# One transformer block, four edits at once: modulation weights as whole rows in a single first pass, value rows padded to 320 bytes, a reordered end of attention, and feed-forward weights in three slots queued by ScalarE

## The chip, the cores and the metric

The kernel runs on one core of a Trainium2 chip. The metric is device time in microseconds (us) of one execution; lower is better. Every number below comes from timed runs or from profiles (hardware traces of one execution). Engines: PE is TensorE (matrix multiply), PEld its weight loads, DVE VectorE, ACT ScalarE, POOL GpSimd, SP SyncE, which issues DMAs.

## The reference, cut to what matters

```python
mod = silu(c) @ w_mod            # c: 1x1024, w_mod: 1024x6144 -> sa, ca, ga, sb, cb, gb
h = layernorm(x) * (1 + ca) + sa # x: 2048x1024, bf16
x = x + ga * A(h)                # A: q = h @ wq (32 heads of 128), softmax(q k^T) v over the last
                                 #    512 cached keys (4 key heads, 8 query heads each), then @ wo
h = layernorm(x) * (1 + cb) + sb
x = x + gb * B(h)                # B: (silu(h @ w_gate) * (h @ w_up)) @ w_down, inner width 3584
```

The first product that needs `h` needs `sa` and `ca`, which are 2048 columns of `w_mod`: 4 MB that must arrive before the block can begin.

## The kernel before

Work is done in four chunks of 512 rows of x. Four parts matter here.

**The start.** The modulation columns come in two slices, and so does the first projection of four heads. `mod_slice` is 32 one-column matmuls per half slice; `x_mod` turns the transposed, normalized x into `hT`.

```python
# c arrives transposed, as 1024 pieces of 2 bytes
SP.dma_start(cT_bf[:, :], c.rearrange("o (k p) -> p (k o)", p=P))
...
for sl in range(2):
    load_wme(sl)          # four DMAs of 512 KB, runs of 1 KB
    load_wq0(sl)          # half of the first projection weights
...
for sl in range(2):
    if sl == 1:
        warm(4, SCB + 1); mod_slice(1, 0); warm(2, SCB + 1); mod_slice(1, 1)
        x_mod(1)
    for kc in range(sl * HK, (sl + 1) * HK):
        for h in range(LEAD + 1):
            mm(bank(QB0[h]), wq_s[0][:, kc, h*P:(h+1)*P], hT[0][:, kc, :], ...)
```

`warm(n, b)` is n matmuls of zeros, 512 columns each, whose result nobody reads: they keep PE's clock up.

**The heads.** For each head PE does 8 projection matmuls and 4 score matmuls of 512 columns, and 16 of 129 columns that multiply the exponentials with the value rows. A value row has 128 values and a 1 (for the softmax sum); the rows lie `VW` elements apart.

```python
VW = 130                                   # 260 bytes from row to row
v_aug = arena.at(OFF_VA, [GK, VW], BF16, [B_va])
...
mm(bank(b, P + 1, jj * 130), ex_s[es][:, kt, j*P:(j+1)*P],
   v_aug[:, gk * KT + kt, 0:P + 1], ...)   # 129 columns move through PE
```

**The end of attention.** When no projection is left to overlap, pieces of the last output projection fill in.

```python
if 0 <= i - 1 < NA: scores(i - 1)
n = i - (NA - LEAD)
if 0 <= n <= 2: oproj_mm(NCH - 1, 0, QB, 8 * n, 8 * n + 8)
elif n == 3:    oproj_mm(NCH - 1, 1, XB, 0, 12)
if 0 <= i - 2 < NA: pv(i - 2)
...
oproj(NCH - 1, 3)      # pieces 3 to 7, alternating between two PSUM banks
```

**Feed-forward weights.** Two slots of 2 MB (gate and up), queued by SP, in whose queue layer-norm transposes and output stores stand too.

```python
if jf % 4 == 1 and jf > 4:
    load_wgu(jf // 4 + 1)
gateup(jf)
```

The softmax here doesn't subtract the row's maximum and nothing guards it: scores larger than these inputs give would overflow.

## Time and profile before

1289.8 us median of 3 runs (1289.48 to 1290.48). One profiled execution spans 1289.0 us.

| stage | us from the start | what PE does |
|---|---|---|
| start | 0 to 31.4 | first work at 9.9, first projection in halves at 16.0 and 25.2, done at 30.5 |
| attention, four chunks | 31.4 to 657 | one head every 3.51 us |
| last output projection | 657 to 705 | 512-column matmuls |
| feed-forward | 705 to 1286 | 512-column matmuls |

The page's first part, busy time of each engine with its share of the span, says where to look:

```profile
PE 1263.4 (98%) x7636; PEld 648.3 (50%) x7778; DVE 447.5 (35%) x823; ACT 341.3 (26%) x384; POOL 37.3 (3%) x94
```

PE is busy 98% of the time, and the chain of waits puts 96% on one line of matmuls. So no other engine's speed matters by itself; there are the idle and the slow stretches of PE to win. The groups of instructions by shape (busy time, mean ns of one, idle before them and who ended it):

```profile
L266 PE MATMUL ps<-arena 128*128 128x512 bf16 x5084 | 1134.7, 380 | 11.7 <-DVE arena L467 2.2 <-DMA arena<-in_B_w_up_dram 0.8 <-ACT arena L620 0.7
L266 PE MATMUL ps<-arena 128*128 128x129 bf16 x2048 | 138.5, 220 | 1.1 <-DVE arena L641 1.1
```

A matmul is shown as 380 ns long although the chain steps on by 10.79 us for every 50 of them, 216 ns each: they overlap.

The timeline of PE at the start (start, duration, engine, line, operation; in brackets the idle time before and what ended it):

```profile
9.92 1.03 PE L270 MATMUL ps<-arena,nsc 128*128 128x128 bf16 x8 [9.92 <-DVE nsc L399]
...
16.00 5.47 PE L266 MATMUL ps<-arena 128*128 128x512 bf16 x19 [0.47 <-DVE arena L467]
21.31 0.94 PE L266 MATMUL ps<-sc_bf,arena 128*128 128x1 bf16 x32
22.33 0.38 PE L266 MATMUL ps<-arena 128*128 128x512 bf16 x1
22.55 0.94 PE L266 MATMUL ps<-sc_bf,arena 128*128 128x1 bf16 x32
25.20 5.30 PE L266 MATMUL ps<-arena 128*128 128x512 bf16 x16 [1.71 <-DVE arena L467]
30.34 1.06 PE L270 MATMUL ps<-arena 128*128 128x128 bf16 x16
```

The second half of the projection, 16 matmuls, takes 5.30 us instead of 16 x 0.216 = 3.5. The sums by stretch show why (for each stretch: length, busy time of PE, PEld, DVE, ACT and POOL with counts, granted TensorE clock, busy share of the DMA engines, GB/s):

```profile
10.00:16.00 6.00, 5.41 (x96) 5.20 (x98) 3.98 (x11) 1.73 (x2) 2.17 (x6) 1.00 1.09 385
16.00:22.00 6.00, 6.00 (x47) 2.84 (x47) 0.00 (x0) 0.96 (x2) 0.00 (x0) 1.00 1.09 382
24.00:28.00 4.00, 2.80 (x7) 1.04 (x8) 1.40 (x5) 1.45 (x2) 0.00 (x0) 0.66 0.68 162
```

In 24 to 28 us the granted clock is 0.66 of full speed. And the DMA runs flat at about 383 GB/s from 10 to 22 us.

The end of attention, timeline of PE:

```profile
640.02 14.64 PE L266 MATMUL ps<-arena 128*128 128x512 bf16 x112 [0.45 <-ACT arena L620]
655.75 14.03 PE L266 MATMUL ps<-arena 128*128 128x129 bf16 x74 [1.09 <-DVE arena L641]
670.16 42.05 PE L266 MATMUL ps<-arena 128*128 128x512 bf16 x190 [0.39 <-DVE tmp L660]
```

Three waits, 1.93 us. And in the feed-forward one wait, in the chain that ended last (start, duration, what):

```profile
1026.74 0.55 DVE nsc L399
1027.29 0.02 issue
1027.31 1.23 SPq L418
...
1028.63 0.53 SPq L767
...
1029.26 9.77 DMA arena<-in_B_w_up_dram
1039.03 0.04 issue
1039.08 6.00 PE ps L266 x27
```

SP stood at a layer-norm transpose (L418) until VectorE had made its input, and only then could it issue the gate and up weights behind it; the up weights landed at 1039.03, just too late for PE.

Lastly the pace of the heads, by two starts of a head's reciprocal on VectorE, six heads apart in the third chunk:

```profile
404.94 0.18 DVE L638 RECIPROCAL rl<-ps 128x4 f32<-128x4 f32 x1 [1.09 <-PE ps L266]
...
425.99 0.18 DVE L638 RECIPROCAL rl<-ps 128x4 f32<-128x4 f32 x1 [1.09 <-PE ps L266]
```

21.05 us for six: 3.51 us a head.

### The profile page before, as it was taken

The numbers are of one execution on the slowest core, as the hardware profiler recorded it, in microseconds if no ns is written. First come the engines' busy times: TensorE is split into PE (matmuls) and PEld (weight loads), VectorE is DVE, ScalarE is ACT, GpSimd is POOL, SyncE is SP. The second block draws the span as 40 slices with busy tenths as digits, with TensorE's granted clock in tenths as the row PEclk, the third lists the DMA queues.
The fourth block names the chain that finished last, engine by engine and source line by source line (L and its number), as shares of the span: only waits on it lengthen the run. The fifth ranks groups of instructions, "written<-read, shape, count | busy, mean of one in ns | idle before, by whom it ended". The sixth has DMA issues, their size and how long they took to land.

```text
span 1289.0 us, 17912 instructions
## 1 busy us (share of the span) xinstructions
PE 1263.4 (98%) x7636; PEld 648.3 (50%) x7778; DVE 447.5 (35%) x823; ACT 341.3 (26%) x384; POOL 37.3 (3%) x94
## 2 busy tenths in 40 slices
PE   6999999999999999999999999999999999999999
PEld 3565545665446554455544444444444444444444
DVE  3455424554136542265422331233222331221222
ACT  2555402555015551055520111011100111001100
POOL 1001200000000000000000000000000000000000
PEclk9999999999999999999999999999999999999999
DMA  8999701844105641055341683045410564044300
GB/s 263 311 222 295 218 1 25 193 103 106 34 9 127 143 104 45 1 125 114 70 152 33 194 296 130 17 149 162 149 56 28 151 206 131 17 136 142 131 9 25
DMA packets 212592, 155.33 MB, mean 120 GB/s; under 512 B 104736, under 2 KB 199840, under 8 KB 211488
## 3 DMA queue, kind: packets, MB, share of 16 engines
q1 hardware_dynamic: 212512, 154.17, 42.2%
q8 instruction: 61, 1.00, 0.3%
q14 instruction: 19, 0.16, 0.0%
HBM read 125.83 MB, written 4.19 MB: 101 GB/s over the span
## 4 chain that ended last, share of the span: by engine, by line
PE 97%; DMA 1%; issue 1%; DVE 1%; SPq 0%; ACT 0%; POOL 0%; DVEq 0%
PE ps L266 96%; DMA arena<-in_B_w_up_dram 1%; DMA x_res<-in_A_x_dram 0%; PE ps L270 0%; ACT arena L620 0%; DVE tmp L660 0%; DVE nsc L399 0%; DVE arena L467 0%; DVE st L388 0%; SPq L418 0%; ACT arena L489 0%; SPq L309 0%; DVE arena L641 0%; DVE x_res L662 0%; DVE rl L638 0%
## 5 line engine op out<-in xcount | busy, mean ns | idle before, releaser
L266 PE MATMUL ps<-arena 128*128 128x512 bf16 (+1 forms) x7204 | 1249.3, 333 | 12.8 <-DVE arena L467 2.2
L266 PEld LDWEIGHTS ps<-arena 128*128 128x128 bf16 x7346 | 634.0, 98 | 626.8 <-issue 7.1
L620 ACT ACTIVATE arena<-ps 128x1024 bf16<-128x1024 f32 x256 | 261.7, 1023 | 356.9 <-PE ps L266 345.2
L818 ACT ACTIVATE arena<-ps 128x512 bf16<-128x512 f32 x112 | 66.9, 597 | 515.6 <-PE ps L266 512.8
L819 DVE TENSOR_TENSOR arena<-ps,arena 128x512 bf16<-128x512 f32 x112 | 77.4, 691 | 277.4 <-PE ps L266 277.4
L660 DVE TENSOR_TENSOR tmp<-ps,rowb 128x512 f32<-128x512 f32 (+1 forms) x65 | 44.4, 683 | 320.5 <-PE ps L266 320.5
L571 DVE CAST arena<-ps 128x512 bf16<-128x512 f32 x124 | 85.7, 691 | 65.5 <-PE ps L266 65.5
L641 DVE TENSOR_TENSOR arena<-ps,rl 128x512 bf16<-128x512 f32 x128 | 88.5, 691 | 4.5
L638 DVE RECIPROCAL rl<-ps 128x4 f32<-128x4 f32 x128 | 23.3, 182 | 147.7 <-PE ps L266 147.7
L388 DVE BATCH_NORM_STATS2 st<-x_res 128x6 f32<-128x512 bf16 x62 | 42.4, 683 | 3.9 <-DMA x_res<-in_A_x_dram 3.8
L393 POOL TENSOR_SCALAR rstd<-mv 128x1 f32<-128x1 f32 x31 | 7.0, 227 | 952.8 <-DVE mv L392 941.4
L662 DVE TENSOR_TENSOR arena<-tmp,x_res 128x512 bf16<-128x512 f32 (+1 forms) x33 | 22.3, 676 | 1.1
L662 DVE TENSOR_TENSOR x_res<-tmp,x_res 128x512 bf16<-128x512 f32 x32 | 22.2, 692 | 1.1
L404 DVE TENSOR_SCALAR arena<-arena,gain,mod_bf 128x512 bf16<-128x512 bf16 x56 | 20.3, 405 | 0.0
L395 POOL TENSOR_TENSOR rstd<-rstd,mhalf 128x1 f32<-128x1 f32 x31 | 17.7, 573 | 2.6
L399 DVE TENSOR_SCALAR nsc<-x_res,mv,rstd 128x1024 bf16<-128x1024 bf16 x30 | 16.1, 536 | 2.1 <-POOL rstd L395 2.1
L270 PE MATMUL ps<-arena,nsc 128*128 128x128 bf16 x16 | 2.1, 311 | 10.0 <-DVE nsc L399 9.9
L266 PE MATMUL ps<-sc_bf,arena 128*128 128x1 bf16 x384 | 11.5, 164 | 0.0
L266 PEld LDWEIGHTS ps<-sc_bf,arena 128*128 128x128 bf16 x384 | 11.3, 97 | 0.5
L540 POOL TENSOR_SCALAR arena<-arena,c 128x128 bf16<-128x128 bf16 x16 | 9.7, 620 | 35.9 <-PE ps L266 35.7
L392 DVE BATCH_NORM_AGGREGATE mv<-st 128x2 f32<-128x12 f32 x31 | 6.5, 208 | 1.1
L270 PEld LDWEIGHTS ps<-arena,nsc 128*128 128x128 bf16 x16 | 1.5, 141 | 10.1 <-DVE nsc L399 10.1
(37 smaller groups left out, 30.8 us busy)
## 6 DMA issues: line engine op xcount, KB each, us to landing
arena<-in_A_wq_dram SPq DMA_DIRECT2D x31, 1024.0 KB, 6.0
arena<-in_B_w_gate_dram SPq DMA_DIRECT2D x28, 1024.0 KB, 5.4
arena<-in_B_w_up_dram SPq DMA_DIRECT2D x28, 1024.0 KB, 7.5
arena<-in_w_mod_dram SPq DMA_DIRECT2D x8, 1024.0 KB, 8.0
arena<-in_A_wo_dram SPq DMA_DIRECT2D x8, 1024.0 KB, 8.1
arena<-in_B_w_down_dram SPq DMA_DIRECT2D x7, 1024.0 KB, 6.3
arena<-in_w_mod_dram SPq DMA_DIRECT2D x8, 512.0 KB, 7.8
out_dram<-arena SPq DMA_DIRECT2D x15, 256.0 KB, 2.0
```

What stands on the lines that cost most here:

```text
L266: T.op(PE, lambda: TE.matmul(out_ap, lhsT, rhs, start=start, stop=stop, skip_group_check=skip), reads=reads, writes=[bank_buf])
L388: T.op(DVE, lambda: V.bn_stats(st_[sl][:, hf * 6:hf * 6 + 6], x_res[:, t, hf * 512:hf * 512 + 512]), reads=[B_x[t]], writes=[B_st[sl]])
L395: T.op(POOL, lambda: g.tensor_tensor(rstd[sl][:, :], rstd[sl][:, :], mhalf[:, 0:1], ALU.pow), reads=[B_rs[sl], B_mh], writes=[B_rs[sl]])
L404: T.op(DVE, lambda: V.tensor_scalar(dst[:, dt, :], dst[:, dt, :], gain[gi][:, dt:dt + 1], mod_bf[:, ccol + dt:ccol + dt + 1], op0=ALU.mult ...
L571: T.op(DVE, lambda: V.tensor_copy(qT_s[qs], bank(QB)), writes=[PB[QB], B_qT[qs]])
L620: T.op(ACT, lambda: A.activation(ex_s[es][:, 2 * kp:2 * kp + 2, :], banks2(SCB + 2 * kp), AF.Exp, scale=att_scale), writes=[PB[SCB + 2 * k ...
L638: T.op(DVE, lambda: V.reciprocal(rl[r][:, :].rearrange("p (a b) -> p a b", a=2), psap(PVB * 512 + P, [[512, 2], [130, 2]])), writes=both + ...
L641: T.op(DVE, lambda: V.tensor_tensor(o_s[os_].rearrange("p (a b) d -> p a b d", a=2), psap(PVB * 512, [[512, 2], [130, 2], [1, P]]), rlb, A ...
L660: T.op(DVE, lambda: V.tensor_tensor(tmp[s][:, 0:n], bank(b, n), rowb[ri][:, c0:c0 + n], ALU.mult), reads=[B_row[ri]], writes=[PB[b], B_tmp ...
L662: T.op(DVE, lambda: V.tensor_tensor(dst[:, c0:c0 + n], tmp[s][:, 0:n], x_res[:, t, c0:c0 + n], ALU.add), reads=[B_tmp[s], B_x[t]], writes= ...
L818: T.op(ACT, lambda: A.activation(sg_s[ss], bank(gb), AF.Silu), writes=[PB[gb], B_sg[ss]])
L819: T.op(DVE, lambda: V.tensor_tensor(guT[:, ft, :], bank(ub), sg_s[ss], ALU.mult), reads=[B_sg[ss]], writes=[PB[ub], B_gu[ft]])
```

## The change

Four edits, each with its own aim: let the first projection run in one piece at full clock with larger DMA runs; pad the value rows; fill the idle pieces at the end of attention; and fetch feed-forward weights a group earlier, out of SP's queue. The core of the diff, with cuts marked:

```diff
-    return SP.dma_start(cT_bf[:, :], c.rearrange("o (k p) -> p (k o)", p=P))
+T.op(Q_c, lambda: SP.dma_start(c_row[:, :], c.rearrange("o (k p) -> (o k) p", p=P)), writes=[B_cT])
+T.op(PE, lambda: TE.transpose(bank_bf(XB)[:, 0:DT], c_row[:, :], ident[0:DT, 0:DT]), ...)
 ...
+for k in range(DT):     # whole rows: runs of 4 KB
+    T.op(dq("q_wm%d" % k), lambda: SP.dma_start(wme[k], w_mod[k * P:(k + 1) * P, 0:NE * P]), ...)
-for sl in range(2):
-    load_wme(sl)
-    load_wq0(sl)
+load_wq0(0)
+load_wq0(1)
 ...
-VW = 130
+VW = 160
 ...                     # GpSimd's order: rstd of tiles 0 and 1 now ahead of tile 3's mean
+warm(9, WB)             # then stats, norm, x_first(0), warm(6), x_first(1), warm(2)
+for k in range(3):
+    mod_k(k)
+    warm(2, WB)
 ...
+mod_k(3)
+x_first(3)
+for k in range(4, DT):
+    warm(3, WB)
+    mod_k(k)
+warm(5, WB)
+x_mod()                 # all eight modulations, 5 on VectorE, 3 on ScalarE
 ...                     # the split in the first projection is gone
+n = i - (NA - LEAD)
+if 0 <= n <= 2:
+    oproj_mm(NCH - 1, 0, QB, 8 * n, 8 * n + 8)
+elif n >= 3:
+    oproj_mm(NCH - 1, 1, XB, 8 * (n - 3), 8 * (n - 3) + 8)
 if 0 <= i - 1 < NA:
     scores(i - 1)
-n = i - (NA - LEAD)     # was here, with 12 instead of 16 for piece 1
 ...
-oproj(NCH - 1, 3)
+for k, b in ((3, SCB + 1), (4, QB), (5, XB), (6, SCB + 2), (7, QB)):
+    oproj_mm(NCH - 1, k, b, 0, Hq)
+    oproj_end(NCH - 1, k, b)
 ...
-NWG = 2
+NWG = 3
-    T.op(Q_wg[sl], lambda: SP.dma_start(        # and the same for the up weights
+    T.op(Q_wg[sl], lambda: A.dma_start(
 ...
-if jf % 4 == 1 and jf > 4:
-    load_wgu(jf // 4 + 1)
 gateup(jf)
+if jf % 4 == 0:
+    load_wgu(jf // 4 + 2)
```

More of the change, by code (lines that the diff above doesn't have):

```diff
@@ L181, in bass_adaLN_cond__sliding_block_cached__swiglu_ffn__prompt_kernel @@
     mhalf = S_("mhalf", [P, TPC], F32)
-    cT_bf = S_("cT_bf", [P, DT], BF16)
+    c_row = S_("c_row", [DT, P], BF16)
     sc_bf = S_("sc_bf", [P, DT], BF16)
@@ L188, in bass_adaLN_cond__sliding_block_cached__swiglu_ffn__prompt_kernel @@
     nmean = S_("nmean", [P, 1], F32)
-    nmr = S_("nmr", [P, 1], F32)
     acc = S_("acc", [P, 2], F32)
@@ L232, in bass_adaLN_cond__sliding_block_cached__swiglu_ffn__prompt_kernel @@
     B_cT = _Buf("cT"); B_sc = _Buf("sc"); B_modbf = _Buf("modbf"); B_c6 = _Buf("c6")
-    B_mode = [_Buf("mode%d" % i) for i in range(2)]; B_gf = _Buf("gf")
-    B_nm = _Buf("nmean"); B_nr = _Buf("nmr"); B_acc = _Buf("acc")
-    B_g = [[_Buf("g0_%d" % i) for i in range(2)], [_Buf("g1")] * 2]
+    B_mode = _Buf("mode"); B_gf = _Buf("gf")
+    B_nm = _Buf("nmean"); B_acc = _Buf("acc")
+    B_g = [_Buf("g%d" % i) for i in range(2)]
     B_row = [_Buf("row%d" % i) for i in range(2)]
@@ L294, in _ @@
             T.op(POOL, lambda: g.memset(zwarm, 0.0), writes=[B_zw])
-            def dma_c():
-                with nc.allow_non_contiguous_dma(reason="tiny transposed c load"):
-                    return SP.dma_start(cT_bf[:, :], c.rearrange("o (k p) -> p (k o)", p=P))
             def load_x(ch):
@@ L306, in _ @@
             T.op(Q_x[0], lambda: SP.dma_start(x_res[:, 0, :], xf[0:P, :]), writes=[B_x[0]])
-            T.op(Q_c, dma_c, writes=[B_cT])
+            T.op(Q_c, lambda: SP.dma_start(c_row[:, :], c.rearrange("o (k p) -> (o k) p", p=P)), writes=[B_cT])
             for t in range(1, TPC):
@@ L326, in _ @@
             HK = DT // 2
-            B_wme = [[[_Buf("wme%d%d%d" % (sl, pt, kh)) for kh in range(2)] for pt in range(2)] for sl in range(2)]
-            wme = [[arena.at(OFF_OT + (2 * sl + pt) * 8 * KB, [DT, 512], BF16, B_wme[sl][pt]) for pt in range(2)] for sl in range(2)]
-            def load_wme(sl):
-                for kh in range(2):
-                    for pt in range(2):
-                        c0 = pt * D + sl * 512
-                        T.op(dq("q_wm%d%d%d" % (sl, pt, kh)), lambda: SP.dma_start(
-                            wme[sl][pt][:, kh * HK:(kh + 1) * HK, :],
-                            w_mod[kh * HK * P:(kh + 1) * HK * P, c0:c0 + 512].rearrange("(k p) n -> p k n", p=P)),
-                             writes=[B_wme[sl][pt][kh]])
+            B_wme = [_Buf("wme%d" % k) for k in range(DT)]
+            wme = [arena.at(OFF_OT + k * 4 * KB, [NE * P], BF16, [B_wme[k]]) for k in range(DT)]
+            for k in range(DT):
+                T.op(dq("q_wm%d" % k), lambda: SP.dma_start(wme[k], w_mod[k * P:(k + 1) * P, 0:NE * P]), writes=[B_wme[k]])
             NWQ = 2
@@ L378, in _ @@
                      writes=[B_vg[gk]])
-            T.op(POOL, lambda: g.memset(v_aug[:, :, P:VW], 1.0), writes=[B_va])
-            T.op(ACT, lambda: A.activation(sc_bf[:, :], cT_bf[:, :], AF.Silu), reads=[B_cT], writes=[B_sc])
+            T.op(POOL, lambda: g.memset(v_aug[:, :, P:P + 2], 1.0), writes=[B_va])
+            T.op(PE, lambda: TE.transpose(bank_bf(XB)[:, 0:DT], c_row[:, :], ident[0:DT, 0:DT]),
+                 reads=[B_cT, B_ident], writes=[PB[XB]])
+            T.op(ACT, lambda: A.activation(sc_bf[:, :], bank_bf(XB)[:, 0:DT], AF.Silu), writes=[PB[XB], B_sc])
             B_ns4 = B_ns + [_Buf("ns2"), _Buf("ns3")]
@@ L405, in modulate @@
                                                   mod_bf[:, ccol + dt:ccol + dt + 1], op0=ALU.mult, op1=ALU.add),
-                     reads=[B_g[gi][dt // HK], cbuf[dt // HK], bufs[dt]], writes=[bufs[dt]])
+                     reads=[B_g[gi], cbuf, bufs[dt]], writes=[bufs[dt]])
             def ln_task(ch, dst, bufs, gi, ccol, cbuf):
@@ L456, in x_first, with x_mod @@
                     transpose(bank_bf(dt // 2)[:, o:o + P], nsc4[t][:, dt * P:(dt + 1) * P], [B_ns4[t]], PB[dt // 2])
-            def x_mod(sl):
-                d0 = sl * HK
-                mod_read(d0, HK, 0, B_mode[sl])
-                mod_read(DT + d0, HK, HK, B_mode[sl])
-                mod_gain(0, d0, HK, B_mode[sl], B_g[0][sl])
-                T.op(DVE, lambda: V.tensor_copy(gain_f[:, d0:d0 + HK], gain[0][:, d0:d0 + HK]), reads=[B_g[0][sl]], writes=[B_gf])
-                for dt in range(d0, d0 + HK):
+            def x_mod():
+                T.op(DVE, lambda: V.tensor_copy(mod_bf[:, 0:NE], psap(XB * 512, [[2, NE]])), writes=[PB[XB], B_mode])
+                mod_gain(0, 0, DT, B_mode, B_g[0])
+                T.op(DVE, lambda: V.tensor_copy(gain_f[:, :], gain[0][:, :]), reads=[B_g[0]], writes=[B_gf])
+                for dt in range(DT):
                     src = bank_bf(dt // 2)[:, (dt % 2) * CH:(dt % 2 + 1) * CH]
-                    if dt % 2 == 0:
+                    if dt % 2 == 0 or dt == 5:
                         T.op(DVE, lambda: V.tensor_scalar(hT[0][:, dt, :], src, gain[0][:, dt:dt + 1], mod_bf[:, dt:dt + 1],
                                                           op0=ALU.mult, op1=ALU.add),
-                             reads=[B_g[0][sl], B_mode[sl]], writes=[PB[dt // 2], B_hT[0][dt]])
+                             reads=[B_g[0], B_mode], writes=[PB[dt // 2], B_hT[0][dt]])
                     else:
@@ L472, in x_mod, with mod_k, rstd_pow @@
                                                        bias=mod_bf[:, dt:dt + 1], scale=gain_f[:, dt:dt + 1]),
-                             reads=[B_gf, B_mode[sl]], writes=[PB[dt // 2], B_hT[0][dt]])
-            ECOLS = [(j, j) for j in range(HK)]
-            ECOLC = [(j, HK + j) for j in range(HK)]
-            def mod_slice(sl, kh):
-                for k in range(kh * HK, (kh + 1) * HK):
-                    for pt in range(2):
-                        w = wme[sl][pt]
-                        for j in range(HK):
-                            o = pt * HK + j
-                            mm(bank(XB, 1, 2 * o), w[:, k, j * P:(j + 1) * P], sc_bf[:, k:k + 1],
-                               k == 0 and o == 0, k == DT - 1, [B_wme[sl][pt][kh], B_sc], PB[XB], skip=True)
+                             reads=[B_gf, B_mode], writes=[PB[dt // 2], B_hT[0][dt]])
+            ECOLS = [(j, j) for j in range(NE)]
+            def mod_k(k):
+                mod_mm(wme[k], B_wme[k], k, ECOLS)
             tl = TPC - 1
+            def rstd_pow(t):
+                T.op(POOL, lambda: g.tensor_tensor(rstd[t][:, :], rstd[t][:, :], mhalf[:, 0:1], ALU.pow),
+                     reads=[B_rs[t], B_mh], writes=[B_rs[t]])
             T.op(ACT, lambda: A.activation(nsc4[tl], x_res[:, tl, :], AF.Copy, accum_out=acc[:, 0:1]),
                  reads=[B_x[tl]], writes=[B_ns4[tl], B_acc])
+            WB = PVB
+            warm(9, WB)
+            stats(0, 0, 0)
+            stats(0, 0, 1)
+            aggr(0)
+            stats(1, 1, 0)
+            norm(0, 0, 0)
+            x_first(0)
+            warm(6, WB)
+            stats(1, 1, 1)
+            aggr(1)
             T.op(POOL, lambda: g.tensor_scalar(nmean[:, :], acc[:, 0:1], -1.0 / D, None, op0=ALU.mult),
@@ L494, in _ @@
                  reads=[B_x[tl], B_nm], writes=[B_ns4[tl], B_acc])
-            stats(0, 0, 0)
-            stats(0, 0, 1)
-            aggr(0)
-            stats(1, 1, 0)
-            stats(1, 1, 1)
-            aggr(1)
-            norm(0, 0, 0)
-            x_first(0)
-            mod_slice(0, 0)
+            stats(2, 2, 0)
+            norm(1, 1, 1)
+            x_first(1)
+            warm(2, WB)
+            for k in range(3):
+                mod_k(k)
+                warm(2, WB)
+            stats(2, 2, 1)
+            aggr(2)
             T.op(POOL, lambda: g.tensor_scalar(rstd[tl][:, :], acc[:, 1:2], 1.0 / D, eps, op0=ALU.mult, op1=ALU.add),
                  reads=[B_acc], writes=[B_rs[tl]])
-            T.op(POOL, lambda: g.tensor_tensor(rstd[tl][:, :], rstd[tl][:, :], mhalf[:, 0:1], ALU.pow),
-                 reads=[B_rs[tl], B_mh], writes=[B_rs[tl]])
-            T.op(POOL, lambda: g.tensor_tensor(nmr[:, :], nmean[:, :], rstd[tl][:, :], ALU.mult),
-                 reads=[B_rs[tl], B_nm], writes=[B_nr])
-            T.op(ACT, lambda: A.activation(nsc4[tl], x_res[:, tl, :], AF.Identity, bias=nmr[:, 0:1], scale=rstd[tl][:, 0:1]),
-                 reads=[B_x[tl], B_nr, B_rs[tl]], writes=[B_ns4[tl]])
-            stats(2, 2, 0)
-            stats(2, 2, 1)
-            aggr(2)
-            norm(1, 1, 1)
-            x_first(1)
+            rstd_pow(tl)
             norm(2, 2, 2)
-            mod_slice(0, 1)
             x_first(2)
-            x_first(3)
-            x_mod(0)
+            warm(3, WB)
+            T.op(DVE, lambda: V.tensor_scalar(nsc4[tl], x_res[:, tl, :], nmean[:, 0:1], rstd[tl][:, 0:1],
+                                              op0=ALU.add, op1=ALU.mult),
+                 reads=[B_x[tl], B_nm, B_rs[tl]], writes=[B_ns4[tl]])
+            mod_k(3)
+            x_first(3)
+            for k in range(4, DT):
+                warm(3, WB)
+                mod_k(k)
+            warm(5, WB)
+            x_mod()
             NL = NJ - NE
@@ L576, in _ @@
             for sl in range(2):
-                if sl == 1:
-                    warm(4, SCB + 1)
-                    mod_slice(1, 0)
-                    warm(2, SCB + 1)
-                    mod_slice(1, 1)
-                    x_mod(1)
                 for kc in range(sl * HK, (sl + 1) * HK):
@@ L675, in oproj_end, with oproj @@
                 run_bg(1)
-            def oproj(ch, k0=0):
-                for k in range(k0, 2 * TPC):
+            def oproj(ch):
+                for k in range(2 * TPC):
                     b = [QB, XB][k % 2]
@@ L694, in add_ln2 @@
                     h2s[0] = arena.at(OFF_H20, [DT, CH], BF16, B_h2[0])
-                ln2[ch] = ln_task(ch, h2s[s], B_h2[s], 1, 3 * DT, [B_modbf] * 2)
+                ln2[ch] = ln_task(ch, h2s[s], B_h2[s], 1, 3 * DT, B_modbf)
                 bg.append(ln2[ch])
             LOADX = {3: 1, 19: 2, 40: 3}
-            LOADM = {1 + (3 * k) // 2: k for k in range(DT)}
+            LOADM = {(3 * k) // 2: k for k in range(DT)}
+            load_wml(0)
             MODM = {6 + (3 * k) // 2: k for k in range(DT)}
@@ L714, in _ @@
                         mod_read(NE, NL, 0, B_modbf)
-                        mod_gain(1, 0, DT, B_modbf, B_g[1][0])
+                        mod_gain(1, 0, DT, B_modbf, B_g[1])
                         for ri, jt in ((0, 2 * DT), (1, 5 * DT)):
@@ L730, in _ @@
                     qproj(i + LEAD)
-                if 0 <= i - 1 < NA:
-                    scores(i - 1)
                 n = i - (NA - LEAD)
@@ L735, in _ @@
                     oproj_mm(NCH - 1, 0, QB, 8 * n, 8 * n + 8)
-                elif n == 3:
-                    oproj_mm(NCH - 1, 1, XB, 0, 12)
+                elif n >= 3:
+                    oproj_mm(NCH - 1, 1, XB, 8 * (n - 3), 8 * (n - 3) + 8)
+                if 0 <= i - 1 < NA:
+                    scores(i - 1)
                 if 0 <= i - 2 < NA:
@@ L744, in _ @@
                 run_bg(1)
-            NWG = 2
+            NWG = 3
             OFF_WD = 0
-            OFF_G = [OFF_WQ, OFF_HT]
+            OFF_G = [OFF_WQ, OFF_HT, 56 * KB]
+            OFF_U = [OFF_WQ + 8 * KB, OFF_HT + 8 * KB, 144 * KB]
             OFF_GU = 96 * KB
@@ L755, in _ @@
             B_wu = [_Buf("wu%d" % i) for i in range(NWG)]
-            wg_s = [arena.at(OFF_G[i], [DT, 512], BF16, [B_wg[i]]) for i in range(NWG)]
-            wu_s = [arena.at(OFF_G[i] + 8 * KB, [DT, 512], BF16, [B_wu[i]]) for i in range(NWG)]
-            Q_wg = [dq("q_wg%d" % i) for i in range(NWG)]
-            Q_wu = [dq("q_wu%d" % i) for i in range(NWG)]
+            wg_s = [arena.at(OFF_G[i], [DT, 512], BF16, [B_wg[i]]) for i in range(2)]
+            wu_s = [arena.at(OFF_U[i], [DT, 512], BF16, [B_wu[i]]) for i in range(2)]
+            Q_wg = [dq("q_wg%d" % i, A) for i in range(NWG)]
+            Q_wu = [dq("q_wu%d" % i, A) for i in range(NWG)]
             FG = FT // 4
@@ L766, in load_wgu @@
                 sl = G % NWG
-                T.op(Q_wg[sl], lambda: SP.dma_start(
+                T.op(Q_wg[sl], lambda: A.dma_start(
                     wg_s[sl], B_w_gate[:, fg * 512:(fg + 1) * 512].rearrange("(k p) n -> p k n", p=P)), writes=[B_wg[sl]])
-                T.op(Q_wu[sl], lambda: SP.dma_start(
+                T.op(Q_wu[sl], lambda: A.dma_start(
                     wu_s[sl], B_w_up[:, fg * 512:(fg + 1) * 512].rearrange("(k p) n -> p k n", p=P)), writes=[B_wu[sl]])
@@ L774, in _ @@
             HL = Hq - 4
-            oproj_mm(NCH - 1, 1, XB, 12, HL)
+            oproj_mm(NCH - 1, 1, XB, 16, HL)
             oproj_mm(NCH - 1, 0, QB, 24, HL)
             oproj_mm(NCH - 1, 2, SCB, 0, HL)
-            for k, b in ((0, QB), (1, XB), (2, SCB)):
+            for k, b in enumerate((QB, XB, SCB)):
                 oproj_mm(NCH - 1, k, b, HL, Hq)
                 oproj_end(NCH - 1, k, b)
-            oproj(NCH - 1, 3)
+            for k, b in ((3, SCB + 1), (4, QB), (5, XB), (6, SCB + 2), (7, QB)):
+                oproj_mm(NCH - 1, k, b, 0, Hq)
+                oproj_end(NCH - 1, k, b)
             finish(ln2[0])
+            wg_s.append(arena.at(OFF_G[2], [DT, 512], BF16, [B_wg[2]]))
+            wu_s.append(arena.at(OFF_U[2], [DT, 512], BF16, [B_wu[2]]))
             B_h2[1] = [_Buf("h2_1_%d" % dt) for dt in range(DT)]
```

## The prediction

> **What bounds the kernel now.** TensorE. The page gives PE 1263.4 us busy of 1289.0 (98%), and the chain of waits is 96% matmuls of one line. In steady stretches the chain shows 10.79 us per 50 matmuls of 512 columns, 0.216 us each, and an attention head repeats every 3.51 us; the change touches neither. So only PE's idle and slow time can be won. The waits and the timeline show where it is:
> - Start-up. PE's first work comes at 9.9 us; its first transposes wait for the normalized tile, because GpSimd computes a value that needs x tile 3 before the reciprocal roots of tiles 0 and 1. The projection of the first four heads runs in two halves (16.0 and 25.2 us) and ends at 30.5 us. Between the halves PE does 64 one-column matmuls (about 1.9 us) and waits 1.7 us for VectorE. The second half starts at half clock: weight loads follow each other by 0.43 us, and the granted clock is 0.50 at 26 to 28 us, as the Trainium skill has it ("TensorE: Matmul & The Clock Gate", Part 1: idle PE falls to half rate).
> - DMA moves about 383 GB/s from 5 to 24 us, but only 30 GB/s in 3 to 4 us, where c lands as 2-byte pieces.
> - End of attention: PE idles 0.45 (exp), 1.09 (VectorE) and 0.39 us (residual).
> - Feed-forward: one wait of about 0.8 us for an up weight.
>
> **What changes.** c arrives as 8 rows. All 4 MB of the first modulation weights must land before any modulation. At 383 GB/s, behind 1 MB of x, I estimate the last row block at about 16.5 us. But TensorE's order then decides: from c's arrival (about 3.6 us) 9 warm matmuls at half clock (3.8 us), 29 at 0.216 (6.3 us), 128 one-column ones (32 take 0.9 us: 3.6 us), 32 transposes (1.8 us): about 19.1 us. Then the cast, gains and first VectorE modulation (1.5 us; 1.7 before) start the projection at about 20.6 us; 32 warm matmuls take 6.9 us: it ends near 27.5 us instead of 30.5. Gain 3.0 us; 5 if DMA, not the warm-ups, were the limit. The start of the attention loop (31.4 to 36.5 us before, with the exp table load) should move along unchanged.
>
> Output projection pieces moved in front of scores, 16 instead of 12 ahead of the last head, and more PSUM banks fill the three idle pieces: about 1.9 us. The third slot removes the 0.8 us. Issuing on ScalarE costs it about 1 us per four blocks of 3.45 us (an issue takes 0.5 us on SyncE); ScalarE is 11% busy there, so no loss. The skill ("DMA: Bandwidth & Descriptors", Issuing engines are not separate DMA queues) says that the engines are the same, so no bandwidth is gained; no trace here shows it yet. 320-byte value rows: nothing, since a head already runs at 3.51 us, nearly 12 x 0.216 + 16 x 0.056.
>
> **Sum.** 3.0 + 1.9 + 0.8 = 5.7 us: 1284.1 us, 80% range 1281.3 to 1287.0. Faster by over 2% 0.01, within 2% 0.97, slower 0.02.
>
> **Right or wrong.** In the profile after: first projection starts at 19.5 to 21.5 us, ends at 26.5 to 28.5 with the granted clock near 1; PE does not wait for modulation rows after the fifth; no idle of PE near 640, 655 and 670 us; no wait for an up weight; head period still 3.51 us.
>
> **What would break it.** Feed-forward weights on ScalarE's queue now start before the last output transposes and share the DMA engines with them; a late transpose would stall PE near 660 us. ScalarE stuck on a full queue would delay the SiLU. PE dropping to half clock between the modulation blocks. Rows landing later than the estimate.

## The result, and the profile after

1283.22 us median of 4 runs (1282.58 to 1284.60) against 1290.14 (1289.48 to 1290.63, 4 runs: the three above and one more). The ratio is 0.9948, 95% interval 0.9931 to 0.9965. Ratios here are the mean time of one kernel's runs over that of the other's of the same rounds, so not quite the ratio of the medians quoted. A ratio of 0.9948 at 1290 us is a gain of 6.7 us; 5.7 had been predicted, and the time lies within the stated range.

Busy time of each engine:

```profile
PE 1273.6 (99%) x7816; PEld 649.6 (51%) x7816; DVE 447.3 (35%) x820; ACT 339.4 (26%) x382; POOL 37.0 (3%) x93
```

The timeline of PE at the start:

```profile
3.72 3.49 PE L265 MATMUL ps<-arena 128*128 128x512 bf16 x9
...
18.33 0.54 PE L265 MATMUL ps<-sc_bf,arena 128*128 128x1 bf16 x16
18.73 1.24 PE L265 MATMUL ps<-arena 128*128 128x512 bf16 x5
20.25 7.15 PE L265 MATMUL ps<-arena 128*128 128x512 bf16 x32 [0.28 <-DVE arena L454]
27.24 1.06 PE L269 MATMUL ps<-arena 128*128 128x128 bf16 x16
```

The first projection starts at 20.25 and its 32 matmuls are through in 7.15 us, 0.22 each: full clock. The next work begins at 27.24 instead of 30.34. The same stretches as before:

```profile
10.00:16.00 6.00, 6.00 (x112) 4.26 (x110) 1.09 (x2) 0.10 (x2) 1.68 (x4) 1.00 1.02 412
16.00:22.00 6.00, 5.72 (x69) 2.99 (x68) 2.82 (x8) 1.44 (x2) 0.00 (x0) 1.00 1.09 352
24.00:28.00 4.00, 4.00 (x30) 2.23 (x29) 0.80 (x2) 0.56 (x1) 0.00 (x0) 1.00 0.99 243
```

While the modulation rows arrive (10 to 16 us) the DMA moves 412 GB/s instead of 385. (This trace holds no clock records, so its 1.00 for the clock is no evidence; the spacing of the matmuls is.)

From 86.56 us on PE never idles as far as the trace tells; one line of its timeline reaches over the whole of attention and into the feed-forward (the view ends at 720 us):

```profile
86.56 633.64 PE L265 MATMUL ps<-arena 128*128 128x512 bf16 x4292
```

So the three waits near 640, 655 and 670 us are gone in this execution, and no up weight is waited for later. (Six other traces have both the new end of attention and ScalarE's queue; in three of them a new, smaller wait stands near 660 us. See b_ffn.) And the heads' pace:

```profile
400.96 0.18 DVE L626 RECIPROCAL rl<-ps 128x4 f32<-128x4 f32 x1 [1.08 <-PE ps L265]
...
421.94 0.18 DVE L626 RECIPROCAL rl<-ps 128x4 f32<-128x4 f32 x1 [1.08 <-PE ps L265]
```

20.98 us for the same six heads (21.05 before): 3.497 us a head instead of 3.508. That is small, but there are 128 heads, and the prediction had said that this would not change.

Where this pair of traces differs, by the same event in both: 3.11 us at the first head's reciprocal (38.01 and 34.90), 4.61 at the 121st (632.16 and 627.55), 7.11 at the first product of the feed-forward (708.41 and 701.30), 8.25 at the end. So the start gave 3.1, the heads 1.5, the end of attention 2.5 and the feed-forward 1.1 us. That is 8.2 us where the timed runs show 6.7: one pair of traces can't be the whole story, and the experiments had to find which of these numbers belong to the change and which to that one execution.

### The profile page after: what moved, and what is told of

It is laid out like the page before. It is cut to its first block, busy times and chain, and to the rows that moved or that the text cites. A ratio compares the mean times of both kernels' runs of the same rounds, so it can differ in the third digit from the quotient of the medians.

```text
span 1280.8 us, 18074 instructions
## 1 busy us (share of the span) xinstructions
PE 1273.6 (99%) x7816; PEld 649.6 (51%) x7816; DVE 447.3 (35%) x820; ACT 339.4 (26%) x382; POOL 37.0 (3%) x93
## 4 chain that ended last, share of the span: by engine, by line
PE 99%; DVE 0%; ACT 0%; DMA 0%; issue 0%; POOL 0%; ACTq 0%; DVEq 0%
PE ps L265 98%; DMA x_res<-in_A_x_dram 0%; PE ps L269 0%; ACT arena L608 0%; DVE st L377 0%; ACT L608 0%; POOL rstd L384 0%; DVE nsc L388 0%; ACT arena L581 0%; POOL rstd L382 0%; DVE arena L454 0%; DVE mv L381 0%; DVE tmp L648 0%; DVE arena L650 0%; DVE mod_bf L448 0%
## 5 line engine op out<-in xcount | busy, mean ns | idle before, releaser
L265 PE MATMUL ps<-arena 128*128 128x512 bf16 (+1 forms) x7383 | 1264.3, 334 | 0.5 <-DVE arena L454 0.3
(39 smaller groups left out, 27.9 us busy)
```

Source lines behind the costliest of these rows:

```text
L265: T.op(PE, lambda: TE.matmul(out_ap, lhsT, rhs, start=start, stop=stop, skip_group_check=skip), reads=reads, writes=[bank_buf])
```

## The experiments

Twelve kernels ran, all with correct results. The first four put one part of the change alone into the kernel before; the four cuts add up to the whole change exactly. Medians below are beside runs of the kernel before on the same chip.

### b_start: the new start alone

Edit: the kernel before with c as rows, whole modulation rows, one pass, the warm matmuls and the early first late-modulation load; everything else as before.

> The kernel before with the new start alone (c as rows, whole modulation rows, one pass, warm matmuls, early first late-modulation load). Theory: the start is worth what the profile shows at the end of the first projection, 30.5 to 27.4 us, so the time falls by about 3.1 us and the head period stays 3.51 us. Rival (prediction's own alternative, DMA as the only limit): 5 us. If the start also shifts something later, the gain at the end of the program differs from the gain at 27 us.

Measured: 1287.53 us (1286.97 to 1287.78, 5 runs) against 1289.51; ratio 0.9983 (0.9970 to 0.9997), 2.2 us less. In its trace the first head's reciprocal is at 35.39 us, not 34.90. So I compared all traces, by that same event. With the old start: 38.01, 37.33, 36.57, 37.34, 38.79, 37.54 us, mean 37.6. With the new start unaltered: 34.90, 35.39, 34.85, 35.41, mean 35.1. The start is worth 2.5 us; the 3.1 of the first pair was a slow old start beside a quick new one. The rival's 5 us is out. One of nine runs of the kernel before shows a mean granted clock of 1.000 in place of 0.999, and it took 1287.18 us, 2.3 less than their median: a hint, from one run, that most of what the old start loses hangs on its 3.4 us at half clock. The pieces of the new start (c as rows, whole rows, one pass, warm matmuls, GpSimd's order) were not tried one by one; a_nowarm and a_1kb bear on two of them.

### b_pitch: 320-byte value rows alone

```diff
-VW = 130
+VW = 160
```

> The kernel before with 320-byte value rows alone. Theory: the attention-value matmuls run 0.8 ns faster each (57.5 to 56.7 ns), 2048 of them, so the head period falls from 3.51 to 3.50 us and the time by 1.6 us. Prediction on record: nothing, period stays 3.51. Rival: the shorter period in the changed kernel comes from somewhere else, and this run keeps 3.51.

Measured: 1288.80 us (1287.45 to 1288.97, 5 runs) against 1289.51; ratio 0.9992 (0.9979 to 1.0004): too small for the timing to show by itself. The trace shows it plainly. Its heads are 3.497 us apart, as in the changed kernel, and not 3.508; in b_start, b_tail and b_ffn, which keep 260 bytes, they stay 3.508 apart. From start to start its 129-column matmuls are 56.7 ns apart, all 16 of a head alike. In the kernel before, each value row serves two matmuls in a row, and on three rows out of four the first of the two is 59 to 61 ns from the second; the mean is 57.5 to 57.9. From the first head's reciprocal to the 121st it is 592.65 us here and in the changed kernel, and 594.15 or 594.16 in the kernel before and in b_start, b_tail and b_ffn: 1.5 us in 120 heads, 12.5 ns a head, 1.6 us for 128. The prediction's "nothing" fell here.

### a_mix: four row pitches in one kernel

Each of the four key heads has its own pitch, so that one execution compares them.

```diff
-VW = 160
-v_aug = arena.at(OFF_VA, [GK, VW], BF16, [B_va])
+VPITCH = [130, 132, 136, 160]      # 260, 264, 272, 320 bytes
+v_flat = arena.at(OFF_VA, [GK * 160], BF16, [B_va])
+def v_group(gk):                   # each group starts at a multiple of 1280 bytes
+    p = VPITCH[gk]
+    return v_flat[:, gk*640 : gk*640 + KT*p].rearrange("p (k w) -> p k w", k=KT)
```

> The changed kernel with another row pitch for the value rows of each key head: 260, 264, 272 and 320 bytes. Theory of 16 bytes: a value row that does not start at a multiple of 16 bytes costs about 4 ns at every second matmul; so the mean spacing of the attention-value matmuls is about 57.4, 57.0, 56.7 and 56.7 ns for the four (260: three of four rows off; 264: two of four; 272 and 320: none). Rival, whole 64-byte lines: 272 bytes is as slow as 260 (57.4) and only 320 is fast.

Measured (one look, 1283.38 us): mean spacing of the 129-column matmuls 57.5 ns at 260 bytes, 57.3 at 264, 56.7 at 272, 56.7 at 320. By row, what counts is where a row starts: rows 4, 8, 12 or 24 bytes into a 64-byte line cost 3 to 5 ns, rows 0, 16, 32 or 48 bytes into it cost nothing. So 16 bytes is the grain; whole 64-byte lines are out, and 272 bytes would have done as well as 320. The reciprocals of heads in the first group (260 bytes) and in the third (272), six heads apart:

```profile
380.23 0.18 DVE L632 RECIPROCAL rl<-ps 128x4 f32<-128x4 f32 x1 [1.09 <-PE ps L265]
...
401.27 0.18 DVE L632 RECIPROCAL rl<-ps 128x4 f32<-128x4 f32 x1 [1.09 <-PE ps L265]
...
436.29 0.18 DVE L632 RECIPROCAL rl<-ps 128x4 f32<-128x4 f32 x1 [1.08 <-PE ps L265]
...
457.27 0.18 DVE L632 RECIPROCAL rl<-ps 128x4 f32<-128x4 f32 x1 [1.08 <-PE ps L265]
```

21.04 us against 20.98. (264 bytes was expected at 57.0; its two bad rows cost nearly 5 ns each, a little more than a bad row at 260 bytes. Why was not tried.)

### b_tail: the end of attention alone

Edit: the reordered output projection and the additional banks, as in the diff above; the rest as before.

> The kernel before with the reordered output projection at the end of attention and the further PSUM banks alone. Theory: the idle pieces of 0.45, 1.09 and 0.39 us go, so 1.9 to 2.4 us less. Rival: they move elsewhere and less than 1 us is won.

Measured: 1287.14 us (1285.82 to 1288.41, 5 runs) against 1289.51; ratio 0.9980 (0.9968 to 0.9993), 2.6 us less. From the 121st reciprocal to the first feed-forward product: 73.81 us, against 76.25 in the kernel before and 76.26 in b_start. That is 2.44 us. PE's timeline in this stretch is one line, with no wait:

```profile
599.78 112.44 PE L266 MATMUL ps<-arena 128*128 128x512 bf16 x695
```

The predicted 1.9 was the sum of the idle times shown (0.45 + 1.09 + 0.39). The start-to-start distances at these places are 828, 1310 and 767 ns in place of 216, 57 and 216: 2.42 us lost. The difference is the 0.16 us by which a matmul's shown end lies behind the moment when the next could have started, once for each of three waits. The trace alone would have given the right number.

### b_ffn, b_ffn_sp3, b_ffn_act2: the feed-forward weights

b_ffn has three slots on ScalarE's queue in the kernel before. b_ffn_sp3 has the three slots but leaves them to SP; b_ffn_act2 has ScalarE's queue with two slots:

```diff
 # b_ffn_sp3: slots and place of issue
-NWG = 2
+NWG = 3
-if jf % 4 == 1 and jf > 4:
-    load_wgu(jf // 4 + 1)
 gateup(jf)
+if jf % 4 == 0:
+    load_wgu(jf // 4 + 2)
 # b_ffn_act2: the queue
-T.op(Q_wg[sl], lambda: SP.dma_start(
+T.op(Q_wg[sl], lambda: A.dma_start(
```

> The kernel before with the feed-forward weights in three slots queued by ScalarE alone. Theory: only the wait for the up weight near 1039 us goes (0.80 us of PE, 1.14 us in the VectorE products), so 0.8 to 1.2 us less; nothing lost near 660 us. Rival: the weights, now started before the last output transposes, delay these and some of it is lost.

> The kernel before with three weight slots in the feed-forward, still queued by SyncE. The smallest slack (first use of an up weight minus its landing) is -0.7 to 0.7 us in four traces with two slots on SyncE, and over 11 us in four with three slots on ScalarE. If the third slot makes the slack, it is over 8 us here; if the queue makes it, it stays under 3 us.

> The kernel before with two weight slots, queued by ScalarE. The least slack on SyncE belongs to weights issued right behind a layer-norm transpose that waits for VectorE (7 to 8 us late in the trace of before). If that queueing is the cause, ScalarE's queue alone lifts the smallest slack to 4 us or more with two slots; if only the third slot helps, it stays under 2 us.

Measured: b_ffn 1289.83 us (1289.04 to 1290.63, 5 runs) against 1289.51; ratio 1.0001 (0.9988 to 1.0013). No gain, although the trace of before shows 1.1 us lost at this place (matmul starts 1180 and 367 ns apart instead of 216). The other traces explain it. I took, for each group of weights, the time between the landing of the up weights and the moment PE needs them (the SiLU of the group's first block starts then). The smallest such slack in an execution:

| feed-forward weights | traces | smallest slack, us |
|---|---|---|
| two slots, SP (before, b_start, b_pitch, b_tail) | 4 | -0.72, 0.70, 0.45, 0.60 |
| two slots, ScalarE (b_ffn_act2) | 1 | 0.01 |
| three slots, SP (b_ffn_sp3) | 1 | 14.6 |
| three slots, ScalarE (b_ffn, after) | 2 | 13.4, 12.5 |

The old scheme is always on the edge and fell off it in one of four executions, the one shown in the profile before. The length of the feed-forward says the same: from its first product to the end of the program 580.62 us in the profile before, 579.48 in b_start, b_pitch and b_tail, and 579.48 in b_ffn. So the gain is about 1.1 us now and then, not in every run. The third slot alone makes the slack. ScalarE's queue alone does not (the second of the two outcomes that I had expected): it does help the weights that stood behind a transpose (group 17: 4.0 us instead of 0.7 or less), but the tightest ones are then groups 3 and 4, whose loads run beside those of the down weights, and at group 4 PE waited a little (453 ns between starts in place of 216).

The rival came true in part. b_ffn has no new wait near 660 us, but with ScalarE's queue the last transpose of the attention output takes 8.2 us to land, and 2.4 in the kernels that leave the weights to SP: the weights now start before it. With the old end of attention there is room for that. The new end leaves less: in the seven traces that have it together with ScalarE's queue (the changed kernel and all runs named a_) this transpose takes 8.7 to 9.5 us, and in three of them (a_mix, a_nowarm, a_1kb) PE waits for it, 504, 712 and 607 ns between starts in place of 216, so 0.3 to 0.5 us. From the chain of a_nowarm that ended last (start, duration, what):

```profile
653.82 9.46 DMA arena<-arena
663.27 0.05 issue
663.32 0.82 PE ps L265 x3
```

Three slots left to SP together with the new end of attention would have kept both the slack of 14.6 us and the transposes of 2.4 us, as far as b_ffn_sp3 and b_tail tell; that kernel was not run.

### a_fewwarm, a_nowarm: what sets the start

```diff
 # a_fewwarm (in a_nowarm, all seven warm() calls go)
 for k in range(4, DT):
-    warm(3, WB)
+    warm(1, WB)
     mod_k(k)
```

> The changed kernel with 1 instead of 3 warm matmuls before each of the last four modulation row blocks (8 fewer, 1.7 us of PE). Theory of the prediction, TensorE's queue sets the start and DMA has slack: the first projection starts 1.7 us earlier, at 18.5 us, and the time falls by 1.7. Rival, seen in the trace after (last row block lands at 18.0 us, first projection weights at 19.5): at most 0.3 us earlier, with TensorE now waiting for the last row blocks.

> The changed kernel with no warm matmul at all. Theory: the projection starts no later (about 20 us) but at half clock: weight loads 0.43 us apart for some 3 to 4 us, 32 matmuls in 8.5 to 9 us instead of 7.15, so its end and the time are 1 to 2 us later than the changed kernel. Rival, the warm matmuls only fill time: same time within 0.3 us.

a_fewwarm: 1283.54 us (1281.54 to 1284.31, 4 runs), ratio 0.9953 (0.9936 to 0.9969): no gain over the changed kernel's 0.9948. In its trace the projection starts at 19.18, 1.0 us earlier: between the two theories. But in that execution the last row block happened to land at 16.98 us; in the changed kernel's trace at 18.01, where PE took it up at 18.33. So TensorE's queue and the DMA are near each other, and which ends later differs from run to run.

a_nowarm: 1284.82 us (1284.76 to 1285.05, 4 runs), ratio 0.9961 (0.9946 to 0.9976), about 1.6 us slower than the changed kernel, as expected. The projection starts at 20.72 and takes 8.39 us, since PE runs at half clock: weight loads 0.43 us apart until 23.7 us. (Start, duration and idle time of PEld:)

```profile
22.43 0.15 PEld L265 LDWEIGHTS ps<-arena 128*128 128x128 bf16 x1 [0.27 <-issue]
22.86 0.15 PEld L265 LDWEIGHTS ps<-arena 128*128 128x128 bf16 x1 [0.28 <-issue]
23.29 0.15 PEld L265 LDWEIGHTS ps<-arena 128*128 128x128 bf16 x1 [0.28 <-issue]
```

So the warm matmuls do not only fill time. In this trace the first head's reciprocal is at 36.61 us, 1.5 later than the mean of 35.1 with them and only 1.0 earlier than the old start's 37.6; another 0.5 us went at 663 us (the transpose above).

### a_1kb: the same modulation block in 1 KB runs

```diff
-for k in range(DT):
-    SP.dma_start(wme[k], w_mod[k * P:(k + 1) * P, 0:NE * P])
+for k in range(0, DT, 4):
+    for n in range(4):
+        SP.dma_start(wme_all[:, k:k + 4, n * 512:(n + 1) * 512],
+                     w_mod[k * P:(k + 4) * P, n * 512:(n + 1) * 512].rearrange("(k p) n -> p k n", p=P))
```

> The changed kernel with the same modulation block fetched as eight pieces of 1 KB runs (four row blocks by 512 columns) instead of eight whole row blocks of 4 KB runs. Theory: the longer runs raise the DMA rate in this stage from about 385 to 412 GB/s, so here the last piece lands 0.7 to 1.5 us later than 18.0 us and the projection starts that much later. Rival: the rate doesn't depend on the run length, the last piece lands at 18.0 within 0.3 us; the start may still move a little because row blocks 0 to 3 arrive together.

Measured: 1287.34 us (1286.49 to 1287.59, 4 runs), ratio 0.9979. The last piece lands at 19.45 us; in seven traces with whole rows the last one lands at 16.98 to 18.78 us, mean 18.05. From 10 to 16 us:

```profile
10.00:16.00 6.00, 3.53 (x60) 2.25 (x58) 1.09 (x2) 0.08 (x1) 1.68 (x4) 0.93 1.09 349
```

349 GB/s against 412: fetched this way the block comes more slowly, and lands 1.4 us later, as expected. But the rate is not the 385 that the theory had taken from the kernel before, where the runs are 1 KB too. Packets of 1 KB take 46 ns there and 51 ns here, so the length of the runs is not all of it. In the kernel before, a piece lands in one stretch of 4 KB per partition, here in four of 1 KB that lie 4 KB apart. No run separates these causes. The projection starts at 24.84, 4.6 us later, and only 1.4 of that is the landing: TensorE waits 1.14 and 1.25 us for pieces early on, loses its clock, and all the warm matmuls behind them in its queue are late as well. So this run shows a lower rate, not what the higher rate is worth.

### a_same and a_best: a try at a better start

a_same is the changed kernel again. a_best takes a_fewwarm and moves the float copy of the gains behind the first two modulations:

```diff
+# for dt in range(DT): in x_mod
+    if dt == 2:
+        T.op(DVE, lambda: V.tensor_copy(gain_f[:, :], gain[0][:, :]), ...)
-    if dt % 2 == 0 or dt == 5:      # on VectorE
+    if dt % 2 == 0 or dt == 1:
```

> The changed kernel once more, unaltered, to be timed beside the next run and to show how far one execution's start differs from another's. Expected: 1283 us; the first projection starts at 20.2 us, or later if the last modulation rows land after 18.3 us (one of four traces so far: 18.8 us, start at 20.7).

> The changed kernel with 1 instead of 3 warm matmuls before each of the last four row blocks, and with the first two modulations on VectorE ahead of the float copy of the gains (0.2 us off the chain from the last row block to the projection). Theory: the start now follows the last row block's landing (17.0 to 18.8 us so far) by 1.8 us instead of TensorE's queue, so 0.3 to 1.0 us less than the changed kernel in the mean, 1282.4. Rival: the projection's own weights, landing at 19.0 to 20.3 us, bind as well and less than 0.3 us is won.

Measured in the same rounds: a_same 1283.08 us (1282.61 to 1283.59, 5 runs), ratio 0.9946 (0.9932 to 0.9959); a_best 1284.40 us (1282.21 to 1285.58, 5 runs), ratio 0.9955 (0.9942 to 0.9967). Not better: one run is faster than all of a_same's, but four are slower, and they spread over 3.4 us instead of 1.0. Its trace shows how the theory failed. PE's timeline:

```profile
15.93 0.54 PE L265 MATMUL ps<-sc_bf,arena 128*128 128x1 bf16 x16
18.26 0.59 PE L265 MATMUL ps<-sc_bf,arena 128*128 128x1 bf16 x16 [1.78 <-DMA arena<-in_w_mod_dram]
18.71 10.95 PE L265 MATMUL ps<-arena 128*128 128x512 bf16 x36
29.50 1.06 PE L269 MATMUL ps<-arena 128*128 128x128 bf16 x16
```

The last row block landed at 18.21 us. With so few warm matmuls left PE had nothing to do for 1.78 us, its clock fell, and the five warm matmuls and the projection then ran at half clock (weight loads 0.43 us apart until 24.5 us). The projection ended near 29.7 instead of 27.9 us in a_same. The clocks of the five timed runs bear this out: 1282.21 us at a mean granted clock of 1.000, 1283.73 and 1284.40 at 0.999, 1284.84 and 1285.58 at 0.997. The three warm matmuls per row block are a bridge over late rows: they cost about 1 us when the rows are early (a_fewwarm's trace, 19.18 against 20.25) and save nearly 2 us when they are late. The changed kernel stands; no version that was timed here beats it.

## Why the prediction was right or wrong

The sum was right: 5.7 us predicted, 6.7 measured, inside the range. The terms, against their parts alone:

| part | predicted | shown by traces | timed alone |
|---|---|---|---|
| start | 3.0 | 2.5 (3.1 in the first pair) | 2.2 |
| value rows | 0 | 1.6 | 1.0 (interval -0.5 to 2.7) |
| end of attention | 1.9 | 2.4 (0.3 to 0.5 less in three of the seven traces that also have ScalarE's queue) | 2.6 |
| feed-forward weights | 0.8 | 1.1 in one execution of four | -0.1 |
| sum | 5.7 | 6.5 without the last | 5.7 |

- **What bounds the kernel** was right: everything gained is idle or slow time of PE, and PE's share went from 98% to 99%.
- **The start** was right in its times: predicted start of the projection 20.6 and end 27.5 us; measured 20.25 and 27.4. Its reasoning was half right. It had the last row block landing at 16.5 us, with DMA far ahead of TensorE's queue and 5 us to be had if DMA were the limit. It landed at 18.0 in that trace. TensorE took it up at 18.33, and in other executions it landed at 17.0 to 18.8. Both limits lie within about a microsecond of each other, so trimming the queue gains nothing (a_fewwarm, a_best).
- **"320-byte value rows: nothing"** was the step that failed. It reads "a head already runs at 3.51 us, nearly 12 x 0.216 + 16 x 0.056". That sum is 3.488; the missing 22 ns a head were called nothing, and 128 heads make 2.8 us of them. About 12.5 ns of them, 1.6 us in all, were rows off a multiple of 16 bytes. The rest was rounding: with the measured 56.7 and 215.8 ns the sum is 3.497, which is the head period after.
- **The end of attention** was right in its mechanism; the size was the sum of the idle times shown, 1.93, in place of the 2.42 us between starts.
- **The feed-forward wait** was read as a property of the kernel. It was a property of one execution of a kernel with slack near zero. The third slot is a good guard, but worth little in the mean. That ScalarE's issuing costs nothing was right within the noise: b_ffn is not slower. No bandwidth was gained either: the median up weight took 7.5 us to land in b_ffn as before (8.4 in the changed kernel), and the transposes beside the weights landed later, as the Trainium skill has it ("DMA: Bandwidth & Descriptors", Issuing engines are not separate DMA queues): whoever issues, the DMA engines are the same.
- **"A late transpose would stall PE near 660 us"**, the first item under what would break it, did not happen in the profile after, but did in three of the seven traces with the new end and ScalarE's queue, at 0.3 to 0.5 us each. So the fear was right in its mechanism, and the profile after happened to be one of the four without it. The head period, predicted to stay at 3.51, is the one item of the list "right or wrong" that came out wrong in that profile.

Errors in opposite directions (1.6 us too little for the value rows, 0.8 too much for the feed-forward, half a microsecond each way for the other two) largely cancelled, which is luck; the right total does not vouch for the terms.

## What to carry to other kernels

Take PE's loss from the distance between starts of matmuls, not from the idle time shown, and don't round off a gap per head or per tile before multiplying it by their number. Lay rows that move through TensorE at a multiple of 16 bytes (shown here for bf16 rows of 129). Before a wait in one trace is priced, or its absence is called shown, look at the same place in other executions; and where a wait for DMA may come late, cheap filler matmuls that keep the clock up can be worth more than the time they take.

## What the Trainium skill lacked or had wrong

- "SBUF — State Buffer", Operand start alignment, treats where an operand may start as a question of legality and says that its runs timed nothing; a note further down on the page does say that SBUF has lines of 16 bytes and that an access in a new line costs something, but it speaks of strides and gives no figure. "TensorE: Matmul & The Clock Gate" (Part 1, Wait — 56ns, not 53.3ns?) gives a warm matmul N / 2.4 GHz + about 2.5 ns, which works out at 56.3 ns for 129 columns, without a condition on where the rows start. What no page has is the price of a row that starts off a multiple of 16 bytes. Here 129 columns took 56.7 ns with rows at multiples of 16 bytes and 57.5 ns on average at 260-byte pitch, where a misplaced row cost 3 to 5 ns.
- "TensorE: Matmul & The Clock Gate", HAM oscillation, gives the rule "no PE-idle gaps >~3.4µs". In a_best the clock was lost with no gap over 1.78 us between 12 and 18.3 us, and in the kernel before with a wait of 1.71 us before 25.20; what stood around the gaps were mostly one-column matmuls. So a short gap with little work before it was enough in these two traces. (The page goes on to a kernel in which many short idles cost the clock, without a length for them.)
- "DMA: Bandwidth & Descriptors", Where 436 GB/s comes from: about 358 GB/s from HBM for one core is said to bind. Loads here ran at 385 (before) and 412 GB/s (after) for six microseconds. The page's own tables for one core alone reach 425, and it says elsewhere that 358 is each core's share when both of a pair stream; so the sentence is too general, not the figure wrong.
- The same page, Specifications, has 512 bytes as the least transfer for line rate. Packets of 1 KB moved 349 GB/s in a_1kb and 385 in the kernel before, packets of 4 KB 412. So above 512 bytes the way a load is cut still mattered; whether by the length of the runs or by where they land is open.
